# A token mixer behind Linformer attention: the first pair's k and v loaded as float32 on the hardware queues and cast on chip

## The chip, the cores and the metric

The kernel runs on one core of one Trainium2 chip. A core has TensorE (PE, with its weight loads as PEld), VectorE (DVE), ScalarE (ACT), GpSimd (POOL) and SyncE (SP); each works through its own list of instructions in order. Transfers are issued from SP, ACT or POOL and carried by 16 DMA engines that all queues of the core share. The metric is the device time in microseconds of one execution.

## The reference

Attention with projected keys and values, then a mixer over tokens and one over channels. There are 8 batches, 8 heads, 1024 tokens and 64 values a head; k and v are projected from 1024 rows to 64 by E and F.

```python
k_proj = np.einsum('ks,bhsd->bhkd', E, k)
v_proj = np.einsum('ks,bhsd->bhkd', F, v)
scores = scale * np.matmul(q, k_proj.transpose(0, 1, 3, 2))
attn = np.exp(scores)          # behind the maximum's subtraction
attn = attn / (np.sum(attn, axis=-1, keepdims=True) + 1e-09)
x = np.matmul(attn, v_proj)    # then heads side by side: [8, 1024, 512]
h = np.maximum(x.transpose(0, 2, 1) @ w_tok1, 0.0) @ w_tok2
u = x + h.transpose(0, 2, 1)
out = u + np.maximum(u @ w_ch1, 0.0) @ w_ch2
```

All inputs and the output are float32 in DRAM. The kernel computes in bfloat16 with float32 sums.

## The kernel before

The program is a list of jobs, each for one engine, made by the functions of the kernel and then written out in the order that the string `ORDER` holds: two characters a job, the job's number in the order in which the code makes it. `plan` decodes it; the last loop writes the jobs out and pins each engine's instructions to that order. `SPOTS` gives the PSUM bank of each group of sums. `FILLS` names places in the order at which a product of zeros (`blank(zero)`, a 128x512 bfloat16 product into bank 5 that nobody reads) is put ahead of the job; a place that is named twice gets two. Where one engine needs another's result, it waits on a semaphore.

Batch 0 opens the kernel, in four pairs of heads (`GROUPS`). For one pair of heads the jobs are, on the engines named:

- the loads of k, v and q (`load_heads`, L367, issued at L358 from POOL). They cast: float32 in DRAM becomes bfloat16 in SBUF, 512 KB read and 256 KB written for two heads.
- `kv_proj` (L503; its products are L521): 16 products of the pair's k and v with the turned E and F, into one bank, then four copies (L334 on DVE or L336 on ACT) to `kb` and `vb`.
- `k_transpose` (L574) and one copy to `kT`; `q_transpose_pe` (eight products of 128 columns, L618) and one copy to `qT`.
- `scores` (four products, L637), then two exponentials on ACT (L652).
- `attend`: four times two products (L672), each with a reciprocal (L686) into `rdn` and a multiply into `x_sb` (L692) on DVE.

E and F are wanted first. They are loaded as float32 into the tile `o0`, E from SP (L257) and F from ACT (L258), turned by eight float32 products in two groups with an identity that POOL makes (L462; `ident32` lies in the tile `ub0`), and copied to `EFT_sb` in bfloat16, one half by ACT and one by DVE (L465). While that is under way TensorE computes products of zeros: `warm` is one of 512 columns in bfloat16, `warm32` one in float32.

The first pair in the order is heads 2 and 3, then heads 4 and 5, 0 and 1, 6 and 7; POOL issues k2, q2, v2 (the number is the first head of the pair), q4, k4, v4, k0, v0, q0, k6, q6, v6, the two halves of w_tok1, w_tok2, and then the channel weights. Behind the pairs come the token mixer (`token1_part`, L1060, whose products need `x_sb` and w_tok1; `token2_part`, L1092), the turning of its result (L1121) and the channel mixer of batch 0 (L1180 up, L1289 down), which then goes on for all batches with the attention of the next one woven in. The weights of the channel mixer are combined on DVE (L476).

`HWK`, with the value 0, is an older switch that could load k or v of heads 0 and 1 as float32; nothing of it is active. `kv32` are views of the output tiles `o1` and `o2`, unused until the first output.

Of the kernel before, what the change touches and what calls it, by code (L numbers as in the profile page):

```python
# [15 lines left out]
    "0R030T0Q050P0S0408060U070W0V001L0X011M02091E0A1F1G1I1H1J0B1K1N1j1O0C1P1k1c0D1Z1d1Q1e1g1f1h1i0E1R1S1l"  # L16
    "1T1m1W1X0s1U0H0u0w0t0v1n0z0G0x0+1+0F0y0-201-101a1Y24111b1V26250J1812271B19151A1621130I14281C1D1u291o"
    "172S230K2A2T221p1r1q2N2O1v1s2B1t2E1x2P0M2C2U1w2Q1y2V2F1z2R2X2K2W2D2Y2H2G2Z2a2L2I2c2J2b2d2M2l0L2x2m2h"
    "2y2e3B2f2n2i2g2p2o2z3C2q2t2+2-2u2j2r0O302k332v2s0Y37342w310N3L0Z0a353M3d3I3H3D3v323J3N36383R3O0c3E3P"
    "3e0d4c0e3Q3j3K0g3h0f393F3i0b3S3A3f3T3k0h3g3U3-3l3V3G0i3w3X9w3n3W3Y3z4d3m3x3+4u4Y3y4a3p4v4Z403q4g410k"  # L20
    "4w3o5A424x4y0l5B4e0j4h5p4b4f454j464i4k3r5C4z0m43475D5E4l444-0o4m503s4o4n3t4+4p5q525t514B5F4q5r4C495s"
    "530p544D3Z5y3u5w0q5H3bA15x4J3c3a6B5u5I554K5z4r4G4L5K5v4A4H9v5L9x6D484I5+6E0r6F564M6C5-6G6O4N6A606P6Q"
    "626H6I6L4O636561646Z6J674s666K4EA26a57684F6M6b696N4Q0n6f4P6U6g6R6W4R6S6h6Y4U4S6V6c6i6T6X5S4T6d6j6k6u"
    "6l6e5T6m6n6x6+6v5U6o4V6-6y6z716p5a6q4W5G705b725J746r7A73756s765M6t776wA35N7B5O585Q787C5R4t5X5P795Y7J"
    "7F7K7D7G7H7Q7EA57I5Z7L7R5dA759A85eA65VA95fAAA45W5c5h5g5i7V7S5l7TAD7Z7X4X5m5j7a7n5k5n7b7o7W7d5o9z7M7e"
    "7p9-7c7O7q7g7P7r7h7N7f7sAF7i7uAH7Y7lAG7t7m7v7jAJ837wAIANAK7x84ALAOAhAM7z7yAiAP877kAj857U7+88AQAb8986"
    "ARAS8AAcAdAk8BAWAlAm8L9yAZ8CAYAeAT8DAfAaAg8FAUAXAV8M8G8EENB3At7-Az8N8mAEA+8+8i8n8TA-EO8k8oAuAvABAn8H"
    "8U8pB4B5AC8-8q81B0Aq8r92Ao8J90Ap938QArAs8jB6AwB18tB2B795Ax8uB88R8l91Ay8s96B9948v8w9G978x8yBB9H988SBD"
    "999I8KBE9KBCBF8z8WBGEP8VEQ9L9ABABI9N9BBJBH9O9+8X9JBKBNA0BLBO8Y9QBM829MBPBRBSBV8I8aBWBQBTBk9R80BYBXBl"
    "8bBZBUBn9PBc8OBdBa9SBeBfBpBbBh8PBgBmBiER9CBj8ZBo9YEVES9TBr9ZEUBqET8eBs9aEW8f8c9UBu8d9g9W9E9hEYBtC1Bz"  # L30
    "9dEZC2B-9iBwC59VC3BxC69eC48gC89D8hEbC9Bv9bEdC0Ec9c9FEfEj9fCBEeEgEkElCC9jB+EmEhEi9kEn9XEpEr9lC7EoCFCA"
    "By9nCGEsEtCDEq9oCEEu9mCJCHEvEwExCI9r9pCKCXEyEz9qCLCYCME+CNCZEaE-F09sCaILCOCPF19tIMCbDACREXCcF2F4F3Cd"
    "CQ9uF5CeF6CpCfF7FBDCChCSFCDEF9CqDFFADSCiCgFDCrDICTFEDGDJF8FGCjFHFFDHFLDTFICxCkFMFJFPClDUCmFKDLDBDVFQ"
    "FNDDDMFTCVCyINFUFRFODKCnFWDWFXCuDXDNFYCvCzFaCwFVDZFbDQDaC+DRFiFcDODcFSDPFZFdFfFeIPFjFgDdCUFhFlIRDYIT"
    "DkDbISCsIQCWDlFkIUIOC-CoFmFnDeD0CtFoFpDoFqD2DpD1D3FxIXDmD4D6DnIWFzFsFrDrD5FtDqDsFuF-DtD7G0DfDuD8G1Dv"
    "DwF+G2DgG3E0FvG4E1DiDxFwIZE2DyG6IbD+E8G7DjE9IcDzIdGDEAIaE5FyGEG9DhIeGAE6IfD-IhIgGHIiGFIjGIG5GGIkG8IY"
    "GVInE7GKMKIoGBImEBGCGLIsIlECItIuIpGNIqIrIvGOE3IwEDGWE4IxI-GZJ0EEIyGaEFJ1EGIzI+EJEHGXJ5EIJ2GYGcJ3J4GJ"
    "MJGdHQJ7IVJ9J8GbJAD9H8GfGeJBHCGMJCGhJ6JEH9GPJFGiJDGgJJHAHDJGEKHRGQJHJKGRHGJIGTHEHHMLJLMMJNHSJMHUGSHT"
    "HJHVJOGnJPELHFJRHKGjJTEMHXHBJSGlGoJUGpHIJVHMHLJWHNGsGUHYJYHiJQJZHaJXGtHbHOHjJbHPGvJaHmHWJcHnJgJdGwJe"
    "MNGuJfGxGmHZGyMPGkJhHpHcMOJjMRHkMSMQJkGzHlHdHoHqHeJnGqHrJlJoHsGrMVG+HtHuG-JiJzJmH0J+HvH4JpH1JvJsH2H+"  # L40
    "JtJqH3H-HwJxJ-I0JwH5JrK0K1JyJuHyMXK2HxI6MYHgMaK4HzH6I7MZK5HfKBI3I8KCK7MbHhMcK8KDMdQIMeMfKEKFMgMTMhI4"
    "KGK3I5MiK6KIMmI9KJIAMjMkKLIBMnKMK9MoMpKTMlKHKAKUMqI1MrMsQKIDL7MtKXMuMvKZKYIEKKMwL6KVIFKaL8I2IGMxKbMy"
    "KNKWH7ICKdMzKcKeLgM+LAM-IHLBKON0IIN1N3LEN2KfLFKlKgLON5KmLPIJN7KhIKLCN6N8LHMWN4N9LILSL9QHNAKPLQLDNCMU"
    "KiLRNBNDLKLTNENHKRKnLGKjNFLJLVNGKSKqNILLNJLhLMNKLWKrLNNPNLKtNMNQNNKkLiNOKsNSLkNTLYKuKQLZNWLjQJNUNXKw"
    "LlNVKoKvKpNZNRKxNYLUNaNeNbLnNcQLLXNfNdKyKzLaQMNhQOLbNjLmLoNiK+QNLpQPNgQQK-LcLqL0NlLrL2LeL1LsNmLyLtQT"
    "LzLuNnNoL+L3NtLwNxNkM4NyL4NqO9LxL5M5NvOANwNzNuOBM6N+M1NpOCODNrN-OEM2O0NsQVM3O2QWLvO1LdO3M7QXO4O5QYOG"
    "O7OHM8O8QZOFO6M9QaL-OIQdLfOJOLQeQbOKQfMBOMM0QcMCMAQgMDQlQkMFQmMEQnQhORQjP4QUMGP6QiONQRP8OSQoP7P9OXQS"
    "QpQqOVUGPAMHOWQuUFOTPBQvQwOYOUMIQrPCOZQsQtOjPDOaQxQ+PFQyQzObQ-OdR0OcPMOePGOkPNP5PIR1R5PJR3PEOlOPPOPQ"
    "OfPPOrOhR6PHPROsR4R7R2PTR8PSPURAR9RBOoRCPVOpOgUIRFOQRDRGOqPWREPKOtPXPeRJRHOiPfRKRNRLPYRIROOuPLRQPZUH"
    "PiRRPgRcOOPhRSOvRMRTRPRUOwUJRdRVPjRWPaRXUNRfUKRZRYOyULRaRhUMPlRgRbReUOPmPwRiPkRjPnPxRkOzPcPoOmO+PpRl"  # L50
    "RmPyO-PqRnOnRrRoQ2RtOxRvPrQ3RwRpP0Q4RqP1RxP2S7RyPsRzPuUPPbR+P-UQRuPvURS0RsQ0S8S1UUSBUVQ1S9SCS3UWSAQ5"
    "PdUTUXS4SEUYUZUSR-SDSFS2UaSGQ6UbUdS5Q7SJUePtUfUcQ9UgUhSPT3SHSKSQUoQASIUpS6STT2UrUqSUSRT6UsSSQBSWUlUt"
    "QCSXPzUmT7T4P+UnUiQ8TASZUjUkShSLT8UxUuT9QDUvSaUwSVUzQESYU-SiU+V0TBSbT5QFV1TCSNV2QGTDSjUyV4P3TETcScV5"
    "V3TFSpV6SqSdSOV9SfV7VASeTGTdVDSMTKV8THTeSrTIVHTJVBVISmVETLVFVCSnVKTgVLVMThTMSoVJTfVOVGTjTNVPVWTkTOVQ"
    "TiTPVRTlVTSsVNStVUVXTRVSTmTSSgVZVVTQTnVaTuTTToSuSkTpTWTqSwTXSxTYVdVYSySlTsSzTvVeTUSvVbVlTVVgVpVnS+Vf"
    "VqVcS-TwVmVtT0U0VuVoT1W1VhU1W2TaViVwVjVrVxU2W5VkWJW6VvWKTzVyT+WNT-V-W8W0VzU3WOW9W7VsU4WAV+WQTrWPTZWR"
    "WLWSW3WDU5W4X0TtWBWyWTTbWCXIWMWzWVW+WUTxWEX1TyWFU7U6U8WWX4W-U9UBWXWbUAWZX2XaX3UCX5WcXbUDXJX7WYXcWdWH"
    "X6XdWGXMX8WgXNX9WhXPXCXQXAXDXeWiWjXfWaXOXBXEXKXGWmXRXLWIWkXUWlWnXVXhWoWeXiXWXgWqXjWrXmWfXnXkXoXSWsXs"
    "XTWpWtXtXlXHUEXYWuXZXuXpWvXqXFX-XXX+WwXxWxXyXvY9XzXrY0XwY1Y4Y2Y3Y6Y5Y7YAYDY8YBYCYJYFYEYMYGYKYNYHYLYO"
    "YIYPYQ"  # L60
)
SPOTS = (
    "3024101126436327273643040127120236363170420436171063240217145624732113405063774765765024721257605205"
    "6726211311072323401724223063354705252601467407364317023117417326261333177136413604752570156153207422"
    "0717501237102275300221337643164504125123103737627351104724633607633666334154626574653573657273116524"
    "1713476526117451111000431363504562017414020567306256407306640427552552201753173152014723475602015723"
    "0720475332734202200176315612415716323744645200150524671"
)
# [18 lines left out]
APART = (6,)  # L87
PART = 4
PARTS = ((0, 1), (1, 1), (2, 1), (3, 1))
HWK = 0  # L90
SIDES = "AAADADADADDAAAAAAAAADAAAAAAAA"
FMAX = 3.4028234663852886e38

# [1468 lines left out]
```

## Time and profile before

| | us |
|---|---|
| median of three runs | 415.25 |
| the three runs | 414.69, 415.35, 415.25 |
| the profiled execution as listed | 415.69 |
| its span, first instruction to last | 413.9 |

| transfer | issued at, us | us to landing |
|---|---|---|
| E (SP) | 0.74 | 3.2 |
| F (ACT) | 0.76 | 3.8 |
| k of heads 2, 3 (POOL) | 1.28 | 5.2 |
| q of heads 2, 3 | 3.15 | 4.7 |
| v of heads 2, 3 | 3.87 | 6.2 |
| q of heads 4, 5 | 4.59 | 6.7 |
| k of heads 4, 5 | 5.30 | 7.3 |
| v of heads 4, 5 | 6.01 | 7.8 |
| v of heads 0, 1 | 7.44 | 9.0 |
| q of heads 6, 7 | 10.34 | 11.1 |

The granted TensorE clock is 0.999 over the span. Times in the profile count from the span's start. A line of the order of time has the start, the length of the group, the engine, the line of the kernel, the operation, and the tiles written and read; in square brackets stands how long the engine had been idle before, and what released it. In the stages each engine has its busy time and its number of instructions, then follow the granted clock, the mean busy share of the transfer engines (over 1 where packets of one engine overlap) and the GB/s that were written.

### The profile page before, as it was taken

What the parts mean: (1) busy time and instruction counts of PE and PEld (TensorE: products, weight loads), DVE (VectorE), ACT (ScalarE), POOL (GpSimd) and SP (SyncE); (2) the same over time, 40 slices, a digit from 0 to 9 for tenths busy, and PEclk for the clock granted to TensorE, in tenths of its full rate; (3) what the DMA queues carried; (4) which work ended last, traced back from release to release, by engine and by line L of the source; (5) the groups of instructions that cost most, each with busy time, mean ns of one, the idle gap of its engine ahead of it and who ended that gap; (6) DMA issues with size and microseconds to landing.
All of it is one profiled execution on the core that took longest, in us unless ns stands there. A gap on an engine that the chain in (4) does not pass through costs nothing.

```text
span 413.9 us, 9589 instructions
## 1 busy us (share of the span) xinstructions
PE 406.4 (98%) x3909; PEld 344.4 (83%) x3911; DVE 355.9 (86%) x773; ACT 221.9 (54%) x429; POOL 66.8 (16%) x105
## 2 busy tenths in 40 slices
PE   8899999999999999999999999999999999999996
PEld 4489888688888888979988899888988798998896
DVE  2289899779999999989979798898989899988686
ACT  1647884258635664574754646455644745445520
POOL 8544021021102120112001112012100001010010
PEclk9999999999999999999999999999999999999999
DMA  8999999997998897978966869873996212251115
GB/s 153 205 202 204 207 190 192 160 172 170 189 166 168 201 170 143 166 156 156 245 118 127 133 148 178 143 167 89 180 227 118 52 51 103 52 115 39 52 69 187
DMA packets 93755, 61.69 MB, mean 149 GB/s; under 512 B 59024, under 2 KB 89232, under 8 KB 93712
## 3 DMA queue, kind: packets, MB, share of 16 engines
q0 software_dynamic: 35088, 45.09, 55.7%
q1 hardware_dynamic: 58256, 15.47, 22.8%
q8 instruction: 30, 0.49, 0.5%
q10 hardware_dynamic: 368, 0.52, 0.3%
q14 instruction: 13, 0.11, 0.1%
HBM read 59.24 MB, written 16.78 MB: 184 GB/s over the span
## 4 chain that ended last, share of the span: by engine, by line
PE 92%; DMA 4%; DVE 2%; POOL 1%; issue 1%; POOLq 0%; DVEq 0%
PE psum L1289 36%; PE psum L1180 35%; PE psum L991 5%; PE psum L875 4%; PE psum L672 3%; PE psum L521 3%; DMA q_sb<-in_q_dram 3%; PE psum L637 2%; DMA v_sb<-in_v_dram 1%; PE psum L712 1%; PE psum L1060 1%; PE psum L736 1%; DVE u L1105 1%; PE psum L1092 1%; PE psum L618 1%
## 5 line engine op out<-in xcount | busy, mean ns | idle before, releaser
L1289 PEld LDWEIGHTS <-G 128*128 128x128 bf16 x1356 | 130.0, 98 | 18.3 <-issue 3.5
L1289 PE MATMUL psum<-wc_sb,G 128*128 128x256 bf16 (+1 forms) x780 | 101.5, 271 | 0.0
L1180 PEld LDWEIGHTS <-wc_sb 128*128 128x128 bf16 x768 | 73.9, 98 | 10.5 <-issue 2.1
L1202 ACT ACTIVATE G<-psum 128x512 bf16<-128x512 f32 x96 | 56.2, 601 | 44.8 <-PE psum L1180 44.3
L1289 PE MATMUL psum<-wT,G 128*128 128x256 bf16 x576 | 75.6, 273 | 0.1
L1216 DVE TENSOR_TENSOR G<-G 128x512 bf16<-128x512 bf16 (+1 forms) x140 | 69.4, 515 | 0.8
L1180 PEld LDWEIGHTS <-wT 128*128 128x128 bf16 x576 | 55.3, 98 | 7.3 <-issue 0.6
L1180 PE MATMUL psum<-S,wc_sb 128*128 128x256 bf16 x384 | 56.2, 273 | 0.0
L1180 PE MATMUL psum<-S,wT 128*128 128x256 bf16 x384 | 56.0, 273 | 0.1
L1180 PE MATMUL psum<-uT,wc_sb 128*128 128x256 bf16 x384 | 55.5, 273 | 0.0
L1326 POOL DMA_DIRECT2D out_dram<-o x30 | 16.4, 548 | 212.7 <-DVE o L1332 171.2
L692 DVE TENSOR_TENSOR x_sb<-psum,rdn 128x256 bf16<-128x256 f32 (+1 forms) x88 | 46.7, 540 | 1.8
L1332 DVE TENSOR_TENSOR o<-psum,u 128x512 f32<-128x512 f32 x59 | 39.9, 681 | 3.7 <-PE psum L1289 3.3
L1208 ACT COPY ub<-psum 128x512 f32<-128x512 f32 x48 | 28.1, 588 | 23.4 <-PE psum L1180 18.5
L652 ACT ACTIVATE a<-psum 128x512 bf16<-128x512 f32 x64 | 34.9, 603 | 8.5 <-PE psum L637 8.3
L1161 DVE CUSTOM_DVE_ANT_0 G<-psum,ub 128x512 bf16<-128x512 f32 x48 | 32.7, 683 | 6.9 <-PE psum L1180 6.6
L1223 ACT COPY psum<-psum 128x512 f32<-128x512 f32 x48 | 27.6, 579 | 18.6 <-PE psum L1180 13.0
L1161 DVE CUSTOM_DVE_ANT_0 G<-psum,ua 128x512 bf16<-128x512 f32 x48 | 32.6, 684 | 5.3 <-PE psum L1180 4.4
L1208 ACT COPY ua<-psum 128x512 f32<-128x512 f32 x48 | 28.3, 590 | 14.0 <-PE psum L1180 13.6
L1180 PE MATMUL psum<-uT,wT 128*128 128x256 bf16 x192 | 28.7, 273 | 0.0
L358 POOL DMA_DIRECT2D v_sb<-in_v_dram x18 | 13.3, 742 | 75.4 <-PE psum L1180 22.7
L672 PE MATMUL psum<-vb,a 128*128 128x130 bf16 x256 | 25.3, 220 | 0.0
(102 smaller groups left out, 499.4 us busy)
## 6 DMA issues: line engine op xcount, KB each, us to landing
out_dram<-o POOLq DMA_DIRECT2D x30, 512.0 KB, 3.8
k_sb<-in_k_dram POOLq DMA_DIRECT2D x14, 512.0 KB, 11.2
v_sb<-in_v_dram POOLq DMA_DIRECT2D x14, 512.0 KB, 7.3
q_sb<-in_q_dram POOLq DMA_DIRECT2D x14, 512.0 KB, 9.2
wc_sb<-in_moe_w_ch_dram POOLq DMA_DIRECT2D x6, 256.0 KB, 11.9
wc_sb<-in_moe_w_ch_dram POOLq DMA_DIRECT2D x4, 384.0 KB, 13.3
k_sb<-in_k_dram POOLq DMA_DIRECT2D x4, 256.0 KB, 7.9
q_sb<-in_q_dram POOLq DMA_DIRECT2D x4, 256.0 KB, 8.1
```

Of the source, the lines that this page charges most:

```text
L652: lambda g=g, half=half, bk=bk: nc.scalar.activation(out=a_t[g][:, half], in_=bank(bk), func=ACT.Exp, scale=scale),
L672: nc.tensor.matmul(view()[:, k, c].rearrange("p i d -> p (i d)"), a_t[g][:, c, at : at + P], vb[:, g].rearrange("k i d -> k (i d)"), start ...
L692: lambda: nc.vector.tensor_tensor(out=x_sb[:, rows, g * P : (g + 1) * P].rearrange("p (n c) (i d) -> p n c i d", c=2, i=2), in0=view()[:, ...
L991: nc.tensor.matmul(view(X_OF[n])[:, r, :], tok2_of(n, i, r), T[n] if n in T else h[B[n]], start=(n in (1, 7) and r == 0), stop=True, skip_ ...
L1161: nc.vector._custom_dve(TENSOR_ADD_SAT, out=out, in0=in0, in1=in1, s0=FMAX, s1=0.0)
L1180: nc.tensor.matmul(t[:, c, :], w1_of(n, dd, 2 * m + c), a_of(j, n, dd), start=(n in (1, 7) and c == 0 and dd == 0), stop=(c == 1 and dd == 1),
L1202: lambda: nc.scalar.activation(out=G[:, n, cs], in_=view(src), func=ACT.Relu),
L1208: 512, lambda: nc.scalar.copy(out=dst, in_=view("y")), writes=[(name, s % 2)],
L1216: 512 * len(both), lambda: f(out=G[:, n, c], in0=G[:, a, c], in1=G[:, b, c]), ps=False,
L1223: 512, lambda: nc.scalar.copy(out=view("y"), in_=view("x")), takes=[bk["y"]],
L1289: nc.tensor.matmul(to, G[:, G_OF[n], cc, t * P : (t + 1) * P], w2_of(n, cc)[:, cut], start=(n in opens and (t == 0 or alone) and cc == 0), ...
L1332: 512, lambda: nc.vector.tensor_add(out=dst, in0=view(src), in1=u_of(sh, dh)),
```

## The change

k and v of heads 2 and 3 are no longer loaded by POOL with a cast. They are loaded as float32 into `o1` and `o2`, k from ACT behind F and v from SP behind E, and cast to bfloat16 by four new jobs: for each of k and v the first head on DVE and the second on ACT, 512 columns each.

```diff
-    for i, queue in enumerate((nc.sync, nc.scalar)[:HWK]):
-        queue.dma_start(out=kv32[i], in_=(k, v)[i][0, 0:2].rearrange("h (p si) d -> p h si d", p=P))
+    for to, src, queue in zip(kv32, (k, v), (nc.scalar, nc.sync)):
+        queue.dma_start(out=to, in_=src[0, 2:4].rearrange("h (p si) d -> p h si d", p=P))
...
 LOADS = (
-    ("k", 0, 2), ("v", 0, 2), ("q", 0, 2), ("k", 2, 2), ("v", 2, 2), ("q", 2, 2),
+    ("k", 0, 2), ("v", 0, 2), ("q", 0, 2), ("q", 2, 2),
...
+    lead = 0.0
+    pl.add("SPQ", 4.5, 4.5, lambda: None, writes=["EF"], prio=-1003)
+    for i, (name, to) in enumerate((("k", k_sb), ("v", v_sb))):
+        pl.add("SPQ", 7.0 + 1.9 * i, 7.0 + 1.9 * i, lambda: None, writes=[("kv32", i)], prio=-1002 + i)
+        for h in range(2):
+            (act if h else dve)(
+                512,
+                lambda i=i, h=h, to=to: (nc.scalar.copy if h else nc.vector.tensor_copy)(
+                    out=to[:, 2 + h], in_=kv32[i][:, h]
+                ),
+                reads=[("kv32", i)], writes=[(name, 2 + h)], prio=-100 + i,
             )
```

One of the two float32 products of zeros at the start is gone, and the products of zeros named in `FILLS` become 33 instead of 21:

```diff
-    opening = [warm(zero), warm(zero), warm32(), warm32()]
+    opening = [warm(zero), warm(zero), warm32()]
...
-FILLS = (21, 21, 21, 21, 21, 21, 21, 27, 27, 30, 36, 36, 36, 36, 49, 62, 62, 66, 66, 79, 79)
+FILLS = (11, 11, 11, 11, 11, 21, 21, 21, 21, 21, 21, 21, 21, 21, 21, 21, 21, 33, 33, 33, 36, 36, 36, 39, 39,
+    39, 39, 39, 67, 67, 97, 116, 116)
```

`rdn` becomes one tile with a part for each pair of heads of two batches, in place of two that are used in turn:

```diff
-    rdn_t = [tile_of([P, NJ, 2, 2], F32, f"rdn{i}") for i in range(2)]
+    rdn_t = tile_of([P, 2 * HP, NJ, 2, 2], F32, "rdn")
```

`ORDER` is new. Decoded, its first places read as follows beside the old ones (job and engine; "fill" is the number of products of zeros ahead of it):

| place | before | after |
|---|---|---|
| 0 to 9 | warm32, load k2, identities, warm, load q2, warm, warm32, load v2, load q4, load k4 | warm32, (float32 loads), load q2, identities, warm, load q4, warm, load k4 |
| 10 to 20 | turn EF0, load v4, turn EF1, ACT take EF0, load k0, turn q2, DVE take EF1, load v0, DVE take q2, load q0, load k6 | load v4, fill 5 + turn EF1, load k0, turn EF0, load v0, load q0, ACT cast k, DVE cast k, load k6, ACT take EF0, DVE take EF1 |
| 21 to 31 | fill 7 + project 2, load q6, DVE kb and vb of 2, fill 2 + turn k2, load v6, ACT take kT2, fill 1 + scores 2, turn q4 | fill 12 + turn q2, ACT cast v, DVE cast v, load q6, DVE take q2, project 2, turn q4, load v6, DVE kb and vb of 2 |
| 32 to 48 | ACT exponentials of 2, ACT take q4, fill 4 + project 4, attend 2, ACT kb and vb of 4, turn k4, DVE take kT4 | fill 3 + turn k2, ACT take kT2, ACT take q4, fill 3 + scores 2, ACT exponential of 2, fill 5 + project 4, ACT exponential of 2, ACT kb and vb of 4, turn k4 |
| 49 to 68 | fill 1 + scores 4, project 0, ACT kb and vb of 0, fill 2 + turn q0, turn k0, fill 2 + project k6 | scores 4, project 0, ACT kb of 0, ACT exponential of 4, fill 2 + turn q0 |
| 69 to 95 | scores 0, turn k6, fill 2 + turn q6, attend 0, project v6, scores 6 | attend 4, turn k0, project k6, scores 0, turn q6 |
| 96 to 117 | attend 4, first token products | fill 1 + attend 0, turn k6, project v6, scores 6, fill 2 + token products of heads 4, 5 |

Further on the same jobs stand in nearly the same order, with places changed by a few here and there; `SPOTS` changes in the first places and in one bank later.

More of the change, by code (lines that the diff above doesn't have):

```diff
@@ L21 @@
[L21 to L25, printed above, removed]
@@ L656, in scores @@
             )
+    attended = iter(range(2 * B * HP))
     def attend(g, half, due, span):
+        at = next(attended) // 2 % (2 * HP)
         def unit(jn, due):
```

114 lines of the change are left out of this document (53 added, 61 removed).

## The prediction

> **What bounds the kernel now.** I read the page's head first, then the chain of waits, the stages, the transfers and the order of time of the first 26 us, because the diff leaves the rest almost alone.
>
> ```profile
> span 413.9 us, 9589 instructions
> ...
> PE 406.4 (98%) x3909; PEld 344.4 (83%) x3911; DVE 355.9 (86%) x773; ACT 221.9 (54%) x429; POOL 66.8 (16%) x105
> ...
> PE 92%; DMA 4%; DVE 2%; POOL 1%; issue 1%; POOLq 0%; DVEq 0%
> ```
>
> TensorE is the bound: 98% busy, 92% of the chain. What an opening can save is only the time before TensorE is fed without gaps. The chain in order of time shows what rules there:
>
> ```profile
> 3.20 0.67 POOL q_sb L358
> 3.87 6.17 DMA v_sb<-in_v_dram
> 10.04 0.29 issue
> 10.34 11.12 DMA q_sb<-in_q_dram
> 21.46 0.05 issue
> 21.50 0.62 PE psum L618 x8
> ```
>
> The columns are start, length and what. Up to 21.5 us the chain is two transfers: v of the first pair (heads 2 and 3) until 10.04, and the last pair's q until 21.46. The stages give the rate (last column: GB/s written, half of what is read where a cast halves it):
>
> ```profile
> 7.00:8.00 1.00, 0.29 (x5) 0.15 (x4) 0.69 (x1) 0.24 (x1) 1.00 (x2) 1.00 1.10 167
> 8.00:9.00 1.00, 1.00 (x12) 0.65 (x11) 0.41 (x1) 0.00 (x0) 1.00 (x3) 1.00 0.76 122
> ...
> 10.00:12.00 2.00, 1.72 (x24) 0.74 (x24) 1.02 (x4) 0.27 (x1) 1.14 (x2) 1.00 1.23 201
> ...
> 23.56:25.35 1.79, 1.51 (x25) 1.27 (x22) 1.65 (x7) 1.08 (x2) 1.01 (x2) 1.00 1.12 212
> 25.35:28.37 3.02, 3.02 (x57) 3.02 (x55) 2.95 (x15) 1.04 (x3) 1.25 (x2) 1.00 1.40 194
> ```
>
> The transfers run at 122 to 199 GB/s from 4 to 10 us and at 201 or more afterwards. TensorE is gapless only from 25.35. Landings are the issue's start plus the time to landing in the list of issues: E 0.74+3.2=3.9, F 4.6, k of heads 2, 3 at 1.28+5.2=6.5, q 3.15+4.7=7.9, v 3.87+6.2=10.1, q of heads 4, 5 4.59+6.7=11.3, then one every 1.28 (256 KB at 205).
>
> ```profile
> 5.56 1.58 PE L462 MATMUL psum<-ub,o 128*128 128x128 f32 x8
> ...
> 6.66 0.59 ACT L465 CAST EFT_sb<-psum 128x512 bf16<-128x512 f32 x1 [4.03 <-PE psum L462]
> ...
> 7.18 0.69 DVE L465 CAST EFT_sb<-psum 128x512 bf16<-128x512 f32 x1 [5.30 <-PE psum L462]
> ...
> 8.31 1.67 PE L436 MATMUL psum<-zero 128*128 128x512 bf16 x7
> ...
> 9.91 0.24 PE L521 MATMUL psum<-k_sb,EFT_sb 128*64 128x128 bf16 x1
> ```
>
> The second figure is the length. E and F are turned at 5.56, seven products of zeros fill the wait, and the first projection starts at 9.91, when v lands.
>
> **The change part by part.**
>
> Two casting loads leave POOL: 2 x 0.72 us of issue. POOL never holds TensorE up here, so that is worth 0 by itself; the later loads are issued 0.7 to 1.4 earlier, but they queue for the transfer engines anyway.
>
> Two float32 loads go behind E on SP and behind F on ACT. Each issue costs 0.57 (E's row 0.57, F's 0.56). On SP nothing else is due for tens of us; on ACT the table load (1.28, now at 1.35) slides to about 1.9 and ends near 3.2, far ahead of ACT's first work at 6.66. Cost 0.
>
> Their transfer: 512 KB read each, as before, and 512 KB written instead of 256. No row has this transfer alone. Bound from below: the stretch 3.2 to 3.7, when E and F alone flow, has a mean of 420 GB/s, so 1.25 us each, no dearer than the 1.28 of a casting load. Bound from above: 311 GB/s, the mean of the stage from 3 to 4, 1.7 us each. I take 1.28, the row that is nearest in kind. k, v and the first q are then 3.8 us behind F's last byte (4.2, landing 4.6): all three are down by 8.4, or 9.0 if q of heads 4, 5 takes a share. Today the same three take until 10.1.
>
> So the stream gains 1.1 to 1.7 us if the slow stretch from 4 to 10 us is a matter of the casting queue's start, and nothing if it is the engines'. I take 1.2: q of heads 4, 5 lands at 10.1, their v at 12.6 (13.8 now), k and v of heads 0, 1 at 14.0 and 15.2 (16.4 now), q of the last pair at 19 to 20.3 (21.46 now), the first half of w_tok1 at 22.3 (23.5 now).
>
> The Trainium skill (DMA: Bandwidth & Descriptors, "Issuing engines are not separate DMA queues") speaks against this: transfers from scalar, sync and gpsimd share the same 16 engines, so a second issuer saves only issue time. By that rule the stream would not be earlier at all; the rate of 122 in the stage from 8 to 9, with an engine share of 0.76, says that there is slack which the rule leaves out.
>
> Four casts are added, two on each of DVE and ACT, 128x512 from float32 in SBUF. Nearest rows: DVE 0.69 (L465, from PSUM), ACT 0.59. Below: 0.34, the DVE's bf16 512-column rows. ACT takes them in order: cast k, take of E and F, cast v: 3 x 0.6 plus some 0.2 of signalling, 2.0 after k lands. With k at 7.0 to 8.0 that is 9.0 to 10.0. DVE is idle then; cover complete.
>
> TensorE's opening: one float32 product of zeros fewer, about 1.7 (the six opening products span 4.64; two of them are float32), five bfloat16 ones more ahead of the turn, 0.215 each warm (seven span 1.67, six spacings and a last length of 0.38) or twice that cold: 1.1 to 2.1. Turn at 5.0 to 6.0, I take 5.3, done 6.9. Then 12 fills, 2.6, to 9.5; turning q, 8 x 0.057 = 0.45; the first projection at 10.0 to 10.1: **0.15 later than now**. The fills are hidden by the same wait for v as now's seven; if v were there at 8, they would cost up to 1.0.
>
> Then I followed the decoded order through ACT, the engine that now rules. Projection 10.05; ktrans behind three fills at 11.7 (11.37 now); scores 12.4 (11.95); ACT takes qT of heads 4, 5 (1.02) ahead of both exponentials (0.54 each), so these end at 14.45 (13.49 now). The second projection, behind five fills, at 13.75 (13.71). Its four copies on ACT 14.6 to 15.55, scores 16.0 (15.73), projection of heads 0, 1 at 16.4 (16.40 now). From here q, k6 and q6 no longer have to be awaited, but ACT has exponential 0.60, four copies 0.94, exponential 0.60, qT 1.01, kT 0.28 in a row: scores of heads 0, 1 at 20.15 (19.84), q6 turned at 20.4 (21.50), scores of heads 6, 7 at **23.15 (23.22 now)**. So the gates open 1.2 us earlier and ACT gives nearly all of it back.
>
> What is left is the filling behind. Today eight attend products of heads 4, 5 (0.46 us) stand behind the last scores, and of the 1.79 us from 23.56 to 25.35 some 1.2 are work (6 x 0.057 and 16 x 0.055). In the new order those eight are done near 19, with their four DVE reciprocals and multiplies (2.3 us of DVE), and the token products can run gapless from 23.6, as w_tok1 is down at 22.3. At 25.35 the kernel is ahead by 0.46 + 1.79 - 1.2 = 1.05; with 0.05 from the scores, and less 0.1 for w_tok1's second half (24.8 less 1.2, 23.6), **1.0 us**. DVE, busy 2.95 of 3.02 behind that, starts those stages 1.2 earlier and can follow. Afterwards TensorE is the bound, and the lead stays.
>
> A row of rdn for each pair costs and gives nothing: reciprocal and multiply stand in order on DVE anyway. Behind place 277 of 2203 only 14 jobs move by more than three places: 0, within 0.3 either way.
>
> Sum: 413.9 - 1.0 = 412.9 of span. That execution is listed at 415.69, with 1.8 around the span; the median of the three runs is 415.25, so I forecast 415.25 - 1.0 = **414.2**. About 0.2%, 0.83 us, is what a measurement of this kernel can tell from no change.
>
> **The rivals.**
>
> *The stream is no earlier.* The 16 engines are the bound and the slow stretch comes again. For: the engine share is 1.10 to 1.25 in most stages from 5 us on. Against: 0.76 from 8 to 9. Then w_tok1 lands at 23.5 as now, the token products start at 24, and only the 0.46 of attend products is won against 0.15 lost in the first projection: 414.9. The skill's rule quoted above points here.
>
> *The first pair comes late (slower).* v32 and k32 share the engines with POOL's q and the next q. E's row lands before F's by 0.6 although both were issued within 0.02 us: a queue's share seems to go as a whole. If q, v32, q4, k32 go by turns, k is the fourth: 4.2 + 4 x 1.28 + 0.35 = 9.7. ACT's first instruction is k's cast, and the take of E and F and v's cast stand behind it: 11.7, projection 11.9, 1.85 late. ACT's row of work carries that on unshortened; less the 1.0 won, 416.1. It decides from a projection later than about 10.9, that is, k landing later than 8.7. For: strict order on ACT. Against: POOL's q4 is issued only at 3.15 or later.
>
> *More is won.* If DVE casts at 0.34 and v is down by 8, nothing waits, and the earlier loads let weight sums start early enough to remove DVE waits near 31.8 to 37.9: 413.2.
>
> **How the numbers follow.** Forecast 0.48, no earlier stream 0.20, late pair 0.23, more won 0.09. The likeliest one's own range is 413.6 to 414.8; about two thirds of it lies below 414.42. Range over all: from 412.8 (more won, with 0.4 of spread) to 416.3 (late pair). Faster by over 0.2%: two thirds of 0.48, most of the 0.09 and a part of the 0.20: 0.46. Within: 0.29. Slower by over 0.2%: the late pair and a little: 0.25.
>
> **What would show it.** k and v as float32 landing by 9, against 9.7 or later; the first L521 product at 10.1, against 11.9; q6 turned before 20.6; the last scores (L637) at 23.1; L1060 gapless from 23.6. It is wrong if the rate stays below 180 GB/s from 4 to 10 us, if L521 starts after 10.9, or if weight loads now collide with something behind 38 us.

## The result, and the profile after

The changed kernel takes 417.39 us (median of six runs, 416.64 to 418.07) against 415.3 (six runs, 414.69 to 415.6): ratio 1.0052, 95% interval 1.0038 to 1.0065. It is slower by 2.1 us, where 1.0 us less was forecast. The page's head after the change:

```profile
span 414.9 us, 9618 instructions
...
PE 407.5 (98%) x3921; PEld 344.7 (83%) x3921; DVE 357.1 (86%) x775; ACT 222.9 (54%) x431; POOL 65.5 (16%) x103
...
PE 97%; ACT 1%; issue 0%; DVE 0%; DVEq 0%
```

Transfers have gone from the chain of waits (4% before), and the kernel is slower all the same. The order of time of the opening (start, length, engine, line, what, and in brackets the idle time before it with its releaser) shows that most steps of the forecast came true here:

```profile
5.87 1.05 PE L461 MATMUL psum<-ub,o 128*128 128x128 f32 x8
...
6.28 0.62 ACT L385 CAST k_sb<-o 128x512 bf16<-128x512 f32 x1 [3.03 <-DMA o<-in_k_dram]
...
9.36 0.62 ACT L385 CAST v_sb<-o 128x512 bf16<-128x512 f32 x1 [1.81 <-DMA o<-in_v_dram]
...
9.89 0.24 PE L520 MATMUL psum<-k_sb,EFT_sb 128*64 128x128 bf16 x1
...
20.50 0.62 PE L617 MATMUL psum<-ident,q_sb 128*128 128x128 bf16 x8
...
22.87 0.41 PE L636 MATMUL psum<-qT,kT 64*64 64x512 bf16 x4
...
23.65 1.06 PE L1063 MATMUL psum<-x_sb,wt_sb 128*128 128x128 bf16 x16
```

The first projection starts at 9.89 (forecast 10.05), the last pair's q is turned at 20.50 (20.4), the last scores start at 22.87 (23.15), and the token products run almost without a gap from 23.65 (23.6; TensorE is busy for 1.76 of the 1.79 us from 23.56 to 25.35). So the loss had to be looked for behind the opening. To find it I matched the k-th product of one of the two largest groups (L1289 before, L1292 after) with the k-th of the other kernel, and did the same for every later experiment. The offset is how much later a product starts than in the profiled run of the kernel before; a negative one is a lead. The last column is called the closing from here on:

| kernel | offset at 52 us | at 318 us | at 330 us | start of the last product | from there to the span's end |
|---|---|---|---|---|---|
| before | 0 | 0 | 0 | 410.40 | 3.51 |
| after | -0.54 | -0.52 | -0.13 | 410.26 | 4.60 |

After an opening that is 0.54 us ahead, 0.39 us is lost in one place near 320 us, called the stall below, and 1.09 us in the closing. (Part of the opening's lead is gone before 52 us already. Counted by the products done that are not of zeros, it is 0.84 us at 25.35, 0.73 from 36 to 40 and 0.55 at 52; from 33 to 42 us TensorE's weight loads wait 0.5 us for weight sums on DVE, L475, against 0.3 before.) Both places have a line. Near 320 us DVE waits for a turned u, in the changed kernel:

```profile
318.64 0.42 DVE L810 TENSOR_TENSOR S<-uT 128x512 bf16<-128x512 bf16 x1 [0.71 <-DMA uT<-u]
...
320.18 1.47 PE L1292 MATMUL psum<-wT,G 128*128 128x256 bf16 x12 [0.23 <-DVE o L1345]
```

and does not before:

```profile
318.32 0.41 DVE L807 TENSOR_TENSOR S<-uT 128x512 bf16<-128x512 bf16 x1
```

The list of issues from 312 to 315 us (last figure: us to landing) has 6.0 for it after, and 4.4 before:

```profile
uT<-u SPq DMA_TRANSPOSE x1, 6.0
```

```profile
uT<-u SPq DMA_TRANSPOSE x1, 4.4
```

The list of issues behind 408 us has the closing stores, first the changed kernel, then the one before:

```profile
out_dram<-o ACTq DMA_DIRECT2D x2, 128.0 KB, 2.5
out_dram<-o SPq DMA_DIRECT2D x2, 128.0 KB, 2.5
```

```profile
out_dram<-o ACTq DMA_DIRECT2D x2, 128.0 KB, 2.2
out_dram<-o SPq DMA_DIRECT2D x2, 128.0 KB, 2.2
```

The single records of both places tell more. An instruction fetch is a transfer that brings an engine its next instructions. The fetches of 16 KB are taken for TensorE's: the kernel before has 30 of them, one for every 253 or so of TensorE's records.

```
u's transfer near 313 us, landings of its 16 pieces, us from its issue
  before: 4.22 ... 4.33 4.37          TensorE's instruction fetch (16 KB): 3.96, 1.50 long
  after:  4.24 ... 4.36 4.38 5.96     the same fetch:                      3.89, 0.88 long
last store, landings of its last pieces, us from the last product's start
  before: 2.55 2.57 2.58 2.59         after: 2.54 2.58 2.61 3.11 3.30
SyncE's last waits, one on each of eight completion semaphores, in a fixed order
  before: the last one waits for the last store, which is down at 412.99; it ends at 413.01
  after:  the second waits for the last store and ends at 413.58; behind it 413.64 413.70
          413.76 413.82 413.88 413.95
```

So the closing's 1.09 us is a last piece that lands 0.71 us later (3.30 against 2.59), and six further waits of 0.06 us each that before were already done. The semaphores are given to the hardware queues' transfers by turns; two transfers more than before move the stores on by two.

### The profile page after: what moved, and what is told of

It is laid out like the page before. It is cut to its first block, busy times and chain, and to the rows that moved or that the text cites. A ratio compares the mean times of both kernels' runs of the same rounds, so it can differ in the third digit from the quotient of the medians.

```text
span 414.9 us, 9618 instructions
## 1 busy us (share of the span) xinstructions
PE 407.5 (98%) x3921; PEld 344.7 (83%) x3921; DVE 357.1 (86%) x775; ACT 222.9 (54%) x431; POOL 65.5 (16%) x103
## 4 chain that ended last, share of the span: by engine, by line
PE 97%; ACT 1%; issue 0%; DVE 0%; DVEq 0%
PE psum L1183 36%; PE psum L1292 36%; PE psum L994 5%; PE psum L878 4%; PE psum L520 4%; PE psum L675 4%; PE psum L435 3%; PE psum L636 2%; PE psum L1095 1%; PE psum L1063 1%; PE psum L715 1%; PE psum L739 1%; PE psum L617 1%; PE psum L1124 0%; ACT a L651 0%
## 5 line engine op out<-in xcount | busy, mean ns | idle before, releaser
L1292 PEld LDWEIGHTS <-G 128*128 128x128 bf16 x1356 | 130.0, 98 | 18.8 <-issue 3.9
L1292 PE MATMUL psum<-wc_sb,G 128*128 128x256 bf16 (+1 forms) x780 | 101.5, 271 | 0.0
L1183 PEld LDWEIGHTS <-wc_sb 128*128 128x128 bf16 x768 | 73.8, 98 | 10.5 <-issue 2.3
L1292 PE MATMUL psum<-wT,G 128*128 128x256 bf16 x576 | 75.6, 273 | 0.2 <-DVE o L1345 0.2
```

Source lines behind the costliest of these rows:

```text
L1183: nc.tensor.matmul(t[:, c, :], w1_of(n, dd, 2 * m + c), a_of(j, n, dd), start=(n in (1, 7) and c == 0 and dd == 0), stop=(c == 1 and dd == 1),
L1292: nc.tensor.matmul(to, G[:, G_OF[n], cc, t * P : (t + 1) * P], w2_of(n, cc)[:, cut], start=(n in opens and (t == 0 or alone) and cc == 0), ...
```

## The experiments

Time is the median; the ratio is to runs of the kernel before on the same chip. Offsets and closing are those of the one profiled run of each kernel, as in the table above. The text recorded ahead of each run stands before what came of it, and theories A and B are those of that text.

| kernel | us | ratio, 95% interval | offset at 52 us | lost near 320 us | closing |
|---|---|---|---|---|---|
| after_again | 417.16 | 1.0049, 1.0036 to 1.0061 | 0.02 | 0.28 | 4.64 |
| before_lanes2 | 416.38 | 1.0023, 1.0009 to 1.0037 | -0.58 | 0 | 4.47 |
| after_lanes6 | 416.96 | 1.0037, 1.0025 to 1.005 | 0.46 | 0.33 | 4.18 |
| after_pool | 416.62 | 1.0037, 1.0023 to 1.0051 | 0.16 | 0.34 | 3.53 |
| after_1937 | 417.43 | 1.0042, 1.0028 to 1.0057 | -0.39 | 0.43 | 4.62 |
| before_1937 | 415.43 | 0.9992, 0.998 to 1.0004 | -0.36 | 0 | 3.52 |
| after_tail_lanes6 | 416.92 | 1.0031, 1.0019 to 1.0044 | 0.36 | 0.45 | 3.98 |
| after_vfirst | 417.75 | 1.005, 1.0029 to 1.007 | -1.00 | 0 | 4.62 |
| before_count10 | 415.64 | 1.0009, 0.9998 to 1.002 | -0.10 | 0.29 | 3.52 |
| before_sp8 | 415.25 | 0.9997, 0.9986 to 1.0008 | -0.94 | 0 | 3.53 |
| after_vfirst7 | 415.6 | 1.0017, 1.0003 to 1.0032 | -1.44 | 0 | 4.50 |
| after_efpool | 415.12 | 1.0006, 0.9991 to 1.0021 | -1.06 | 0 | 3.50 |
| before_sp7act1 | 415.57 | 0.9999, 0.9989 to 1.001 | -0.81 | 0.25 | 3.63 |
| after_sp8 | 416.76 | 1.0028, 1.0006 to 1.005 | 0.91 | 0 | 3.65 |
| after_vfirst7_sp8 | 415.02 | 0.9993, 0.998 to 1.0006 | 0.06 | 0 | 3.53 |
| after_f23 | 417.62 | 1.0043, 1.0027 to 1.0059 | -0.34 | 0 | 4.54 |
| after_f23_lanes6 | 416.52 | 1.0021, 1.0007 to 1.0035 | 1.14 | 0 | 4.19 |
| after_vfirst7_lanes6 | 414.81 | 0.9986, 0.9976 to 0.9996 | -1.46 | 0 | 3.62 |

### The closing

before_lanes2 gives the kernel before two more transfers on a hardware queue and nothing else; after_lanes6 gives the changed kernel six, so that it has eight more than before and the semaphores come round to where they were:

```diff
+    spare = [tile_of([1, 8], F32, f"spare{i}") for i in range(2)]    # six in after_lanes6
...
+        if place == 2080:                                            # 2084 in after_lanes6
+            for t in spare:
+                nc.sync.dma_start(out=t, in_=E[0:1, 0:8])
+            pin()
```

> The kernel before with two loads of 32 bytes on SP near 390 us, when SP has nothing to do, into tiles that nobody reads: they only move the closing stores on by two of the eight completion semaphores, as the two new loads of the change do. Theory A: the closing waits fall as in the changed kernel, +0.4 to +2.1 us, 415.7 to 417.4. Theory B, and any theory by which the opening or the order costs the time: 415.3, within 0.3.

> The changed kernel with six such loads of 32 bytes, so that the closing stores have the semaphores that they have in the kernel before. Theory A: the loss goes, and the opening's lead of 0.1 to 0.5 is left: 414.8 to 415.3. Theory B: 417.4.

The two loads alone bring the closing from 3.51 to 4.47 and the time to 416.38: half of the change's loss without its opening. With six more on the changed kernel the waits behind the stores are gone, but a late piece stays (3.27 against 2.64 for the one before it): 4.18. So theory A was right about the waits and too narrow about the closing. And it was wrong as a whole, since after_lanes6 still takes 416.96.

after_pool has the changed kernel's order and products of zeros, but POOL loads k and v with a cast, ahead of q; nothing is added to the hardware queues, and the four casts are left out, as the data come cast:

```diff
-    for to, src, queue in zip(kv32, (k, v), (nc.scalar, nc.sync)):
-        queue.dma_start(out=to, in_=src[0, 2:4].rearrange("h (p si) d -> p h si d", p=P))
...
+            lambda i=i, to=to: nc.gpsimd.dma_start(
+                out=to[:, 2:4], in_=(k, v)[i][0, 2:4].rearrange("h (p si) d -> p h si d", p=P)
+            ),
```

> The changed kernel, its order and products of zeros, but k and v of the first pair are loaded by POOL with a cast ahead of the first q, and the four casts are left out. Theory A: the closing is that of the kernel before; the opening loses its earlier stream, v lands near 8.5 and the first q near 9.5, so some 415 to 416. Theory B, where order and products of zeros cost the time: 417 or more.

> The changed kernel once more, for a second trace. Theory A (closing): products are 0.1 to 0.5 us ahead of the kernel before up to the last product, and all that is lost lies behind the last product, where the first profile has 4.6 us instead of 3.4; median 417.4 again. Theory B (body): the second trace shows another stall like the one near 320 us, 0.4 us or more, so that the last product is later than before's 410.4.

Closing 3.53: without the two hardware transfers the closing's loss is gone. The 0.34 us near 320 us are still there, so those do not come from the transfers. after_again is the changed kernel once more: 417.16, with the stall (0.28) and the closing (4.64) again.

before_sp8 and before_sp7act1 add eight small loads to the kernel before, at place 1200, on SP alone or seven on SP and one on ACT. The semaphores stay as they were:

> The kernel before with eight loads of 32 bytes on SyncE's queue at place 1200, near 230 us. The closing stores keep the completion semaphores that they had, so SyncE's last waits come in the order of before; only SyncE's instructions are more. Theory A (the order of the closing waits is the whole closing loss): the closing takes 3.5 us from the start of the last product, 415.3 us. Theory B (part of the loss is one late piece of the last stores, with an 8 KB instruction fetch near it, and comes with another number of instructions): one piece of the last store lands 0.4 to 0.7 us behind the others, the closing takes 3.9 to 4.2 us, some 415.8 us.

> The kernel before with seven loads of 32 bytes on SyncE's queue and one on ScalarE's at place 1200: as many transfers on each queue as in the changed kernel with six loads more. The closing stores keep their completion semaphores. If one transfer more on ScalarE's queue makes the late piece of the last store: one piece of the last store lands 0.4 to 0.7 us behind the others, the closing takes 3.9 to 4.2 us and the time is 415.8. If not (it came with the changed opening): closing 3.5 us, 415.3 us.

No late piece in either (3.53, 3.63). What goes with it in all twenty kernels is an 8 KB instruction fetch: where one starts 1.49 to 1.86 us behind the last product's start (ten kernels) the last store is down 0.47 to 0.76 us later than before; where the first one starts at 2.09 or later (ten kernels) it is not.

What moves that fetch can be read from the number of records (waits and issues included) that each engine's list has in the trace:

| | kernels | records | fetch, us behind the last product's start |
|---|---|---|---|
| SP, as before | 5 | 92 | 2.09 to 2.49 |
| SP, two transfers more | 7 | 94, 95 | 1.49 to 1.72 |
| SP, with six or eight small loads more | 8 | 101 to 103 | none: it comes at 325 to 376 us of the span |
| ACT, few | 13 | 575 to 577 | 3.93 to 5.18 |
| ACT, more | 7 | 578, 579 | 1.68 to 2.09 |

So before_sp8 and before_sp7act1 do not show that the number of instructions is without effect. Their eight loads take SP's fetch far away from the stores (358 us), and with 577 records ACT's is still late (3.94). after_f23_lanes6 (1.79, late piece) has 578 records on ACT, after_vfirst7_lanes6 (3.93, none) has 577. Which engine a fetch serves is read from these counts, and no run was made to move a fetch alone.

### The stall near 320 us

First the order behind the opening was suspected: job 1937 stands eight places earlier at about that time. It was put back alone, moved alone in the kernel before, and then all places behind 300 were put back (with six small loads at place 1200 for the semaphores):

> Job 1937 of the order (numbered as in the kernel before), which the changed order issues eight places earlier, at about 315 us, is put back to its old place; nothing else differs from the changed kernel. Theory A (this one move makes the stall of 0.3 to 0.4 us that the changed order shows between 305 and 330 us): the stall is gone from the trace and the time is 0.35 us below the changed kernel, some 416.8. Theory B (the stall comes from the sum of the small moves or from where the opening leaves the engines): the stall stays and the time with it, some 417.15. Closing as in the changed kernel, some 4.5 us from the start of the last product to the end of the span, by both.

> The converse: the kernel before with job 1937 alone issued eight places earlier. Theory A: a stall of 0.3 to 0.4 us between 305 and 330 us and 415.6 us. Theory B: no stall, 415.25 us. The closing stays at 3.5 us by both.

> The changed kernel with all places behind 300 in the order of the kernel before, and with six loads of 32 bytes on SyncE's queue at place 1200 (near 230 us), so that eight hardware-queue transfers more are issued than before and the closing stores have the completion semaphores that they had. What is left of the change is the opening alone. If the loss is the sum of closing, stall and opening: closing some 3.5 to 3.7 us, no stall near 320 us, and 415.25 plus 0.5 for the later first projection, some 415.75 us. If the opening costs nothing: 415.25. If the closing stores lose by something else than the order of the semaphores (their pieces held up on one ring): the closing stays at 4.2 or more, and the time is 416.5 or more.

Theory A fell: the stall is in after_1937 (0.43) and even with the old order (0.45), and not in before_1937. But it was missing in after_vfirst (below), which has twelve products of zeros fewer than the changed kernel, and that led to TensorE's instruction fetch. In before_count10 TensorE runs ten products more, of one column each, where it waits for E and F anyway:

```diff
         j.fn()
+        if j is opening[1]:
+            for _ in range(10):
+                nc.tensor.matmul(banks[5][:, 0:1], zero, zero[:, 0:1], start=True, stop=True)
```

> The kernel before with ten products of one column (weights of zeros, 128x128 by 128x1) behind the second opening product, where TensorE waits for E and F; their result is never read. The changed kernel has ten products more than the kernel before. Theory A (the stall near 320 us hangs on how many instructions TensorE has run by then, since its instruction fetch of 16 KB then falls on the last piece of a transposed load): the turned u lands 5.9 to 6.0 us after its issue near 313 us instead of 4.3, the products behind 330 us lose 0.3 to 0.45 us against those before 305 us, and the time is 0.35 us over the kernel before, some 415.65. Theory B (the stall comes from the changed opening's loads or order): no stall, 415.3.

The order of time and the issues of before_count10:

```profile
319.01 0.42 DVE L807 TENSOR_TENSOR S<-uT 128x512 bf16<-128x512 bf16 x1 [0.66 <-DMA uT<-u]
```

```profile
uT<-u SPq DMA_TRANSPOSE x1, 5.9
```

The same wait on the same line, 5.9 us instead of 4.4, 0.29 us lost: with ten products more, 310 us earlier and where TensorE waits anyway, the stall is there. (The time, 415.64, is not clear of noise; the trace is.) All seven kernels with ten more products than before have it, and twelve of the thirteen with as many or fewer do not, by one profile of each. The exception is before_sp7act1 (0.25), so something else can bring it about as well.

How the fetch comes in is less clear. Where there is a stall, the fetch starts 3.75 to 3.99 us behind u's issue and is recorded 0.88 to 1.04 us long, and pieces of u land some 1.5 us late. Where there is none, it starts at much the same time (3.81 to 4.02) but is 1.4 to 1.6 us long, or it comes late (4.49, after_f23_lanes6). One piece of 16 is late in after, after_again, after_lanes6 and after_pool, but four are in after_tail_lanes6, five in before_sp7act1, eleven in after_1937 and all 16 in before_count10. One piece held up behind the fetch would explain only the first four. So the number of TensorE's products is shown to bring the stall about; by what way is open.

The converse on the changed kernel, with 23 products of zeros for 33:

```diff
-FILLS = (11, 11, 11, 11, 11, 21, 21, 21, 21, 21, 21, 21, 21, 21, 21, 21, 21, 33, 33, 33, 36, 36, 36, 39, 39,
-    39, 39, 39, 67, 67, 97, 116, 116)
+FILLS = (11, 11, 11, 11, 11, 21, 21, 21, 21, 21, 21, 21, 33, 33, 36, 36, 39, 39, 67, 67, 97, 116, 116)
```

> The changed kernel with 23 products of zeros for 33 (seven for twelve ahead of q's turn, one or three fewer in three places behind it), so that TensorE has run as many as in the kernel before; nothing else is changed. If the number of products makes the stall near 320 us: no stall, the turned u lands 4.3 us after its issue, and the time is 0.35 us below the changed kernel, some 416.9. If the clock falls where TensorE now stands idle ahead of q's turn, or the stall stays: 417.3 or more. Closing 4.5 us by both.

> The same with six loads of 32 bytes on SyncE's queue at place 1200, which give the closing stores the completion semaphores of the kernel before. F stays on ScalarE's queue. If the late piece of the last store comes with the ten products more: closing 3.5 us, and, with no stall, what is left is the opening with q first: 415.7 to 415.9, if v's landing costs 0.5 us. If the late piece is there without them: closing 4.0 us and 416.3.

The stall is gone in both. The time is not better, and the runs of after_f23_lanes6 spread from 415.05 to 418.47. The stages of its profiled run show why (busy time with the number of instructions for PE, PEld, DVE, ACT and POOL, then the granted clock, the DMA share and GB/s):

```profile
8.00:10.00 2.00, 0.04 (x1) 0.00 (x0) 1.03 (x2) 1.10 (x2) 0.17 (x1) 1.00 1.18 239
10.00:12.00 2.00, 1.58 (x27) 1.36 (x28) 1.17 (x3) 0.62 (x1) 0.96 (x2) 0.94 1.24 205
12.00:14.00 2.00, 2.00 (x13) 1.13 (x10) 0.88 (x4) 0.22 (x2) 1.11 (x2) 0.50 1.24 204
```

TensorE waits there for q's first load, whose turn stands first:

```profile
10.08 0.62 PE L617 MATMUL psum<-ident,q_sb 128*128 128x128 bf16 x8 [2.04 <-DMA q_sb<-in_q_dram]
```

The same stages of the changed kernel:

```profile
8.00:10.00 2.00, 2.00 (x16) 1.12 (x15) 0.43 (x2) 0.62 (x1) 0.99 (x2) 1.00 1.22 230
10.00:12.00 2.00, 2.00 (x30) 1.41 (x29) 1.69 (x5) 0.07 (x1) 0.84 (x2) 1.00 1.24 205
12.00:14.00 2.00, 2.00 (x14) 0.57 (x12) 0.00 (x0) 2.00 (x4) 0.97 (x2) 1.00 1.23 203
```

Two us of idle TensorE are followed by a granted clock of 0.50. In the changed kernel products of zeros cover that wait, and the clock stays at 1.00; the price of ten products more is the stall.

### The opening

Seven profiles have the change's load order. In six of them k or v lands at 6.2 to 7.4 and the other only at 9.2 to 9.9 (8.5 and 10.5 in after_f23_lanes6), in all seven the later of the two 0.5 to 0.7 us behind q's first load. Which of them it is changes from run to run: where F's row lands before E's, k is the early one; where E's is first, v is. The packets tell why the second is late. In the changed kernel's profile F's packets start between 2.08 and 3.41 us and E's between 3.18 and 4.04, so the two queues hardly share. k's, behind F, start between 3.81 and 5.96, from 4.04 to 5.13 alone. v's start only between 5.58 and 8.96, beside those of POOL's q, which start at 5.13. The casts of after_f23 on ACT:

```profile
9.32 0.62 ACT L384 CAST k_sb<-o 128x512 bf16<-128x512 f32 x1 [5.79 <-DMA o<-in_k_dram]
9.85 0.58 ACT L463 CAST EFT_sb<-psum 128x512 bf16<-128x512 f32 x1
10.32 0.62 ACT L384 CAST v_sb<-o 128x512 bf16<-128x512 f32 x1
```

Here k is the late one, and the take of E and F and v's cast, v having landed at 6.33, stand behind it: v's products start at 10.99 (10.92 and 11.04 in after_tail_lanes6 and after_lanes6, where k is late too; 10.03, 10.59 and 10.17 in after, after_again and after_1937, where v is). With the change's 33 products of zeros all later products carry it: the offsets at 52 us of the last five are 0.36, 0.46, -0.54, 0.02 and -0.39, a mean of -0.02. Six profiles with the loads of before (before, before_lanes2, before_1937, before_count10, before_sp8, before_sp7act1) have 0 to -0.94, a mean of -0.47. The one run that the forecast was made against is the latest of the six: v of its first pair lands at 10.04 us and its last q at 21.46, in the other five at 8.66 to 9.85 and 19.92 to 20.52. The single values scatter by about 0.4 us around both means. So no win of 1.0 us is there, while a loss of 0.45 is not clear of the scatter.

In the next kernels q's first load is issued behind the identities, at 1.76 instead of 1.27, and q's turn stands behind the first projection. In after_vfirst the seven products of zeros ahead of the projection are named at a place where no TensorE job stands, so none of them is written out, against what its text says. after_vfirst7 has the seven, and 23 in all:

> The changed kernel with the first q load issued behind the identities on GpSimd (1.1 us later), q's turn behind the first projection, and 7 products of zeros for 12 ahead of it. Theory A (the first projection waits for v's float32 load, which shares the engines with q's, and all behind it is a rigid chain): v lands 0.5 to 1 us earlier, the first projection starts at 9.2 to 9.6, the products of every later stage are earlier by the same, and the time is 0.5 us below the changed kernel, some 416.6. Theory B (v's landing is set by its own queue, or q's later landing takes the place of the wait): the main projection stays at 10.0 to 10.6 or the scores of the first pair are later, and the time is 417.2 or more.

> The changed kernel with q's first load behind the identities, q's turn behind the first projection, and 23 products of zeros for 33 (seven ahead of the first projection, where the last such kernel had none), so that TensorE has run as many products as in the kernel before. Theory A (rigid chain behind v's landing; stall by the count of instructions; closing by the two transfers more): first projection near 9.1, offset of the later products against the kernel before -0.8 to -1.0 us, no stall near 320 us, closing 4.6 us, some 416.0 us, and runs within 1.5 us of each other, since TensorE no longer stands idle ahead of the first projection. Theory B: the spread of 415.8 to 419.4 stays (it came from q's later load), or the first projection starts at 9.9 or later and the time is 417 or more.

after_vfirst's profiled run (415.82) is a full us ahead at 52 us, but its runs reach 419.35, with mean clocks of 0.995 to 0.996 in those of 417.6 and more. TensorE stands idle ahead of the projection (7.23 to 8.60 in the profiled run), and 0.996 over 414 us is what 3.41 us at half the clock make. With the seven products the time is 415.6, 1.8 us below the changed kernel but still over the kernel before (ratio 1.0017), with k down at 5.88, v at 8.11 and q at 8.76. The landings are those of theory A; the lead (1.44) is more than it put. The spread is smaller, but four of the twelve runs still lie at 416.5 or more.

Then the closing was to be kept as before. In after_efpool E and F go by POOL, so that there are no more hardware transfers than before; in after_sp8 and after_vfirst7_sp8 F goes by SP behind E (q first, and q behind), with six small loads on SP; in after_vfirst7_lanes6 F stays on ACT:

```diff
-    nc.sync.dma_start(out=EF_rows[:, 0], in_=E)
-    nc.scalar.dma_start(out=EF_rows[:, 1], in_=F)
+    nc.gpsimd.dma_start(out=EF_rows[:, 0], in_=E)    # after_efpool
+    nc.gpsimd.dma_start(out=EF_rows[:, 1], in_=F)
...
+    nc.sync.dma_start(out=EF_rows[:, 1], in_=F)      # after_sp8, after_vfirst7_sp8
```

> As the last one, and E and F are loaded on GpSimd's queue ahead of q, so that k and v stand first on the two hardware queues and the hardware queues carry as many transfers as in the kernel before; five products of zeros ahead of the first projection. If the three causes are right, closing is 3.5 us, no stall near 320 us, k and v land by 7.5 us, the first projection starts at 8.0 to 9.0, and the later products run 1.0 us ahead of the kernel before's profiled run: some 414.3 us, below both kernels. If q, now behind E and F, lands after 10.5 us, the first scores wait for it and the time is 415.3 or more.

> The changed kernel with its own opening (q first), 23 products of zeros for 33 (seven for twelve ahead of q's turn), F loaded on SyncE's queue, and six loads of 32 bytes on SyncE's at place 1200, so that TensorE has run as many products as in the kernel before, ScalarE's queue carries as many transfers, and the stores have their semaphores: what is left is the opening. Closing 3.5 us, no stall near 320 us by both theories. If v's landing sets the opening and its lateness costs 0.5 us against a normal run of the kernel before: 415.7 to 415.9. If the opening as changed costs nothing by itself: 415.3. If F behind E on one queue lands after 5.0 us, E's and F's turn moves by as much, which the products of zeros behind it hide.

> The same, with q's first load behind the identities and q's turn behind the first projection, seven products of zeros ahead of it. If all three causes are right: v lands near 8 us, first projection 8.6 to 9.1, later products 1.0 to 1.4 us ahead of the profiled run of the kernel before, no stall, closing 3.5 us: 414.3 to 414.7, below both kernels. If the runs that were 1.3 us slower in the last two such kernels stay, a third of the runs lie at 415.8 to 416.2. If the closing is still 4.0 us or more, 415.0 or more.

> The kernel with q's first load behind the identities, q's turn behind the first projection, 23 products of zeros, F on ScalarE's queue, and six loads of 32 bytes on SyncE's at place 1200. First projection at 8.6 to 9.1, later products 1.2 us ahead of the kernel before's profiled run, no stall. With closing 3.5 us: 414.5, below both kernels; with a late piece (closing 4.0 us): 415.0. If a third of the runs is 1.3 us slower, as in two of the three such kernels so far, the median still lies below 415.2.

after_efpool turns E and F only at 7.34 (F lands at 7.20) and ends level with the kernel before; it also loses 0.2 us between 233 and 292 us, for a reason that no run shows. In after_sp8 F lands at 7.38, the clock falls to 0.82 in 10 to 15 us, and the time is no measure of the opening, against what was expected. after_vfirst7_sp8 is a draw. after_vfirst7_lanes6 is faster than both kernels, 414.81, if by little. Its opening, from the order of time:

```profile
5.88 0.62 ACT L384 CAST k_sb<-o 128x512 bf16<-128x512 f32 x1 [2.63 <-DMA o<-in_k_dram]
...
8.20 0.62 ACT L384 CAST v_sb<-o 128x512 bf16<-128x512 f32 x1 [1.21 <-DMA o<-in_v_dram]
...
8.87 0.22 PE L519 MATMUL psum<-v_sb,EFT_sb 128*64 128x128 bf16 x1 [0.82 <-ACT v_sb L384]
...
22.83 1.06 PE L1062 MATMUL psum<-x_sb,wt_sb 128*128 128x128 bf16 x16
```

v's products come 1.16 us earlier than in the changed kernel, and the token products 0.82.

## Why the prediction was wrong

- **The opening's path** was right for the run in which k is early: every product named from the first projection on lies within 0.4 us. E and F were turned at 5.87 (5.3 forecast) and k was down at 6.26 (7.0 to 8.0), but v's landing at 9.33 (9.0 at the latest) was what counted. A float32 load was put at 1.28 us and 1.7 at most; k's packets start over 2.2 us. The stream is 1.0 us earlier (q of heads 4, 5 down at 10.30 against 11.3; 1.2 forecast), and ACT gives most of it back in its row of work, as worked out. The Trainium skill (DMA: Bandwidth & Descriptors, "Issuing engines are not separate DMA queues") lets a second issuer save the time of issue alone. The trace does not speak against that as clearly as the prediction supposed: POOL issues this load at 3.13 instead of 4.59, and no run tells the earlier issue from a faster stream (after_pool, with the issue at 4.58, has it down at 10.83).
- **The late pair** was named as the slower rival with its mechanism, k's cast ahead of the take of E and F and of v's cast on ACT. It happens in three of the seven profiles, with nothing in the program to decide it, at about half the size: v's products at 10.9 to 11.0, where 11.9 was put.
- **The term of 1.0 us won** was sized against a run of the kernel before whose last q came late (21.46; 20.28 in before_lanes2). Against that run itself 0.84 us were won at 25.35 and 0.54 at 52, as TensorE waits longer for weight sums from 33 to 42 us; "DVE ... can follow" did not quite hold. Against the six profiles with the loads of before, the changed opening wins nothing and by the means loses 0.17 to 0.45 us: -0.30, the mean of after, after_again and after_1937, or -0.02, the mean of all five, against -0.47.
- **"Behind place 277 of 2203 only 14 jobs move by more than three places: 0, within 0.3 either way"**: taking the moves back won nothing (after_1937, after_tail_lanes6), but the ten products more that TensorE runs were costed only where they stand. They cost 0.28 to 0.45 us near 320 us.
- **"Afterwards TensorE is the bound, and the lead stays"** is the step that failed. The lead stays from 52 to 318 us, where the offset changes by 0.02, and not behind that: the stall takes 0.39 us of it. The closing behind the last product was not looked at: the two loads were costed by their issue and their bytes, not by the two semaphores that they use up and the fetches that they move. It cost 1.09 us.
- **The sum**: 0.17 to 0.45 for the opening, 0.28 to 0.45 for the stall and 1.09 to 1.13 for the closing make 1.5 to 2.0 us; 2.1 and 1.9 (after_again) were measured. The range held only a late pair, not a cost behind TensorE's last product, and so ended at 416.3.
- The table load cost nothing, as forecast (1.97 to 3.25 us on ACT, whose first work is at 6.28), and so did the casts where k is early. No run has rdn's change alone.

## What to carry to other kernels

A step that adds a transfer also takes a completion semaphore, and one that adds instructions moves every later instruction fetch: so look at the closing waits and match products by rank over the whole span before a lead is carried to the end. Size a gain against several profiles of the kernel before, not one, above all where it rests on one late landing. Keep a load that is wanted first clear of other queues' loads: here it was enough to issue POOL's first q at 1.76 instead of 1.27. Where TensorE waits for a load, cover the wait with products of zeros, as two us of idleness were enough to halve the granted clock.

## What the runs showed of the hardware

- Ten products more at the start make a transposed load 310 us later land at 5.9 us from its issue instead of 4.4 (before_count10), with 0.29 us lost. In the eight profiles with such a stall TensorE's 16 KB instruction fetch near it is recorded 0.88 to 1.04 us long, in eleven of the twelve others 1.4 to 1.6.
- A store's last pieces land 0.47 to 0.76 us later in the ten kernels where an 8 KB instruction fetch starts 1.49 to 1.86 us behind the last product, and in none of the other ten. One transfer or one wait more on an engine can decide it (577 or 578 records on ACT).
- SP's closing waits cost 0.06 us each once the store is down; two transfers more on a hardware queue, whether at the start (after) or near the end (before_lanes2), put six of them behind it.
- Two loads issued from SP and ACT within 0.02 us of 0.74 us land by turns, 0.57 to 0.61 us apart in sixteen of seventeen profiles (0.19 in after_pool), and either may be first (E in six of the sixteen, F in ten). With POOL's q issued at 1.27, the load behind the first of them landed at 6.2 to 7.4 and the other at 9.2 to 9.9 in six of seven profiles.
- Granted clock: its records last 3.41 us or a multiple of that. In after_f23_lanes6 TensorE is idle for 2.06 us of the stretch from 8.36 to 11.77, and the clock is 0.50 from 11.77 to 15.19; in after_sp8 it is idle for 1.87 us from 4.96 to 8.37, and the clock is 0.50 from 8.37 to 11.78. Counted on in steps of 3.41 us from the first record, no other of the first eight such stretches of the twenty profiles is idle for more than 1.68 us, and the clock is 1.00 behind all of them. So here somewhat more than half of one stretch was enough. The first record starts at 4.4 to 7.6 us, so the same wait may fall into one stretch or across two, which can be why runs of one kernel differ. The Trainium skill (TensorE: Matmul & The Clock Gate, "What's actually happening") has the clock fall after an idle window of about 3.4 us; here 1.87 us of idleness in such a stretch did it.
